# Moving the third weight load behind the last V, one projection layout for all groups, an earlier third K, and an early exponential table: a streamed attention decode step

## The chip, the cores and the metric

One core of one Trainium2 chip. The metric is the device time of the kernel in microseconds (us), as the median of repeated executions. The profile is one execution; its span is some 2 us shorter than the device time (before: span 669.6, time of that execution 671.42). Before: 671.78 us median of 3 runs (671.24 to 672.15).

## The reference, cut to what matters

```python
# B = 4 rows, H = 32 heads, 4096 cached positions, 128 per head, bfloat16
xn = layernorm(x)                                       # (4, 1, 640)
q = (xn @ wq) -> (4, 32, 1, 128)
scores = q . k_cache * 128 ** -0.5                      # k_cache (4, 32, 4096, 128)
o = softmax(scores) . v_cache                           # v_cache the same size
A = o.reshape(4, 1, 4096) @ wo                          # wo (4096, 640)
return x + A + gated_mlp(xn)                            # small weights, done at the start
```

K and V are 134.2 MB each (4 x 32 x 4096 x 128 x 2 bytes). Everything else together is some 14 MB. One core has to read 282 MB, once.

## The kernel before

A **unit** is K or V of 8 heads of one batch row, 8.39 MB. There are 16 units of each; unit u belongs to group u // 4 (8 heads) and batch row u % 4, so group 3, the last, has K12 to K15 and V12 to V15. `wo`, the weights of the output projection, comes in four parts of 1.31 MB, one for each group. One buffer of five slots holds all that is streamed; a unit takes two slots.

```python
seq = [("k", u) for u in range(B)]          # k0 k1 k2 k3, then v0 k4 v1 k5 ... v11 k15 v12 v13 v14 v15
for u in range(NU):
    seq.append(("v", u))
    if u + B < NU:
        seq.append(("k", u + B))
place = {("k", 0): 3, ("k", 1): 0, ("k", 2): 2, ("k", 3): 0}
for u in range(B, NU):
    place[("k", u)] = 1 if u % 2 == 0 else 0
for u in range(NU):
    place[("v", u)] = 3                     # V12 and V14 share slots 3 and 4
place[("v", NU - 3)] = 1                    # V13
place[("v", NU - 1)] = 0                    # V15
first = {2: 1}                              # which half of a K unit is read first
cuts = {("k", 0): (0, T // 2, T), ("k", 1): (0, T // 2, T), ("v", NU - 1): (0, 128, 192, 224, 240, T)}
```

All these loads go out on one queue, in order, from the sync engine. A load into a slot is issued only when the last reader of that slot is done: for a K unit the 8 VectorE transposes, for a V unit the 64 PE matmuls.

```python
# ... the loop that issues everything
for i, item in enumerate(seq):
    if i + 1 < len(seq):
        load_unit(seq[i + 1])
        key, u = seq[i + 1]
        if key == "k" and u >= 2 * B - 1 and u % B == B - 1:
            load_wo(u // B - 1)             # wo of groups 0, 1, 2 behind K7, K11, K15
    else:
        load_wo(NG - 1)                     # wo of group 3 behind V15, in four pieces
    # ... K unit: 8 transposes and their score matmuls; in the last K of a group also
    #     the selection, the transposing and the projection of the group before
    # ... after the last K of a group: softmax(g)
    # ... V unit: emit_V(u); in the last group also emit_selL(b)
emit_proj(state["oL"], last=True)
```

The softmax of a group is a chain over several engines: the maximum, then four times (exponential on ScalarE, 8 transposes of the exponentials `x` on PE), copies `xd` on VectorE, then fills of the matmul weights `Zb` on ScalarE, then the 64 V matmuls of the group's first unit, in two halves. Groups 0 to 2 project through `oh -> om -> oT -> proj`; the last group has a direct, shorter form:

```python
def emit_selL(b):                            # last group: one matmul and one 128x8 multiplication
    oh = misc_ps([P, HG], F32)
    nc.tensor.matmul(oh[:], lhsT=state["R"][:, b, :], rhs=SelH[:], start=True, stop=True)
    nc.vector.tensor_tensor(out=state["oL"][:, :, b], in0=oh[:], in1=state[("rinv", NG - 1)][:, :, b], op=ALU.mult)
```

Of the kernel before, what the change touches and what calls it, by code (L numbers as in the profile page):

```python
# [8 lines left out]
ACT = mybir.ActivationFunctionType  # L9
ALU = mybir.AluOpType  # L10
# [6 lines left out]
def kernel(  # L17
# [19 lines left out]
    nc = tc.nc  # L37
# [90 lines left out]
        place[("v", u)] = 3  # L128
    place[("v", NU - 3)] = 1
    place[("v", NU - 1)] = 0  # L130
    first = {2: 1}
    cuts = {("k", 0): (0, T // 2, T), ("k", 1): (0, T // 2, T), ("v", NU - 1): (0, 128, 192, 224, 240, T)}
    for g in range(NG):
        u = B * g + B - 1
        if u < NU - 1:
            cuts[("k", u)] = (0, T // 2, T)
            first[u] = 0
    for u in range(B, NU):
        if u not in first:
            first[u] = u % 2  # L140

    def unit(item):
# [9 lines left out]
        for t0, t1 in zip(c[:-1], c[1:]):  # L152
            nc.sync.dma_start(out=dst[:, t0 * Dh:t1 * Dh], in_=src[:, t0 * Dh:t1 * Dh])

    wo_v = A_wo.rearrange("(h p) n -> p h n", p=P)

    wo_q = A_wo.rearrange("(g p c) n -> g p c n", p=P, c=HG)
    wo_t = at_slot(2, HG * NOUT).rearrange("p (c n) -> p c n", c=HG)

    def load_wo(g):  # L160
        if g < NG - 1:
            nc.sync.dma_start(out=wo_t, in_=wo_q[g])
        else:
            for h0, h1 in ((0, 4), (4, 6), (6, 7), (7, 8)):
                nc.sync.dma_start(out=wo_t[:, h0:h1, :], in_=wo_v[:, g * HG + h0:g * HG + h1, :])

    load_unit(seq[0])

# [154 lines left out]
    nc.vector.tensor_tensor(out=uT[:, :, 0:B], in0=z1, in1=t1[:], op=ALU.mult)  # L323


    for fc in range(FC):
        n = P if fc < FC - 1 else FL
        nb = B if fc else 32
        for hf in range(NH):
            nc.tensor.matmul(proj[32 * hf:32 * hf + nb, 0:NO2], lhsT=uT[:n, fc, 0:nb],  # L330
                             rhs=w_out[:n, fc, hf * NO2:(hf + 1) * NO2], start=(fc == 0), stop=False)
# [68 lines left out]
    def softmax(g):  # L400
# [22 lines left out]
        z_fill(g, 1)  # L423
        rowsum = small.tile([P, NE], F32, tag="rowsum")
        nc.vector.tensor_reduce(out=rowsum[:], in_=rs[:], axis=AX.X, op=ALU.add)
        if g < NG - 1:
            cs = misc_ps([G, 1], F32)
            for e in range(NE):
                nc.tensor.matmul(cs[:], lhsT=SelPe[:, e].rearrange("p h e b -> p (h e b)"), rhs=rowsum[:, e:e + 1],
                                 start=(e == 0), stop=(e == NE - 1))  # L430
            rinv = small.tile([G, 1], F32, tag="rinv")
            nc.vector.reciprocal(out=rinv[:], in_=cs[:])
        else:
            ds = small.tile([P, HP, NE, B], F32, tag="ds", bufs=1)
            for e in range(NE):
                nc.vector.tensor_scalar(out=ds[:, :, e, :], in0=SelP[:].rearrange("p (h b) -> p h b", b=B),
                                        scalar1=rowsum[:, e:e + 1], scalar2=1.0 / HP, op0=ALU.mult, op1=ALU.mult)
            cs = misc_ps([P, G], F32)
            nc.tensor.matmul(cs[:], lhsT=ones_f[:], rhs=ds[:].rearrange("p h e b -> p (h e b)"), start=True, stop=True)
            rinv = small.tile([P, HG, B], F32, tag="rinvL", bufs=1)  # L440
            nc.vector.reciprocal(out=rinv[:].rearrange("p h b -> p (h b)"), in_=cs[:])
            oL = small.tile([P, HG, B], BF16, tag="oL", bufs=1)
            state["oL"] = oL
        state[("rinv", g)] = rinv

    def emit_V(v):
# [39 lines left out]
        nc.vector.tensor_copy(out=oT[:], in_=oT_ps[:])  # L486
        state[("oT", g)] = oT

    def emit_proj(oT, last=False):
        for c in range(HG):  # L490
            for hf in range(NH):
                nc.tensor.matmul(proj[32 * hf:32 * hf + B, 0:NO2], lhsT=oT[:, c, :],  # L492
                                 rhs=wo_t[:, c, hf * NO2:(hf + 1) * NO2],
                                 start=False, stop=(last and c == HG - 1))

    def emit_selL(b):

        oh = misc_ps([P, HG], F32)
        nc.tensor.matmul(oh[:], lhsT=state["R"][:, b, :], rhs=SelH[:], start=True, stop=True)  # L499
        nc.vector.tensor_tensor(out=state["oL"][:, :, b], in0=oh[:], in1=state[("rinv", NG - 1)][:, :, b], op=ALU.mult)  # L500

    fill_qz(0)
    for i, item in enumerate(seq):
        if i + 1 < len(seq):
            load_unit(seq[i + 1])
            key, u = seq[i + 1]
            if key == "k" and u >= 2 * B - 1 and u % B == B - 1:
                load_wo(u // B - 1)
        else:
            load_wo(NG - 1)  # L510
        key, u = item
        g, b = divmod(u, B)
        if key == "k":
            done = b == B - 1 and g > 0
            for k in range(8):
                emit_K(u, k)
                if done and k == 1:
                    emit_sel(g - 1)
                if done and k == 2:
                    emit_oT(g - 1)  # L520
                if done and k == 5:
                    emit_proj(state.pop(("oT", g - 1)))
            if b == B - 1:
                if g < NG - 1:
                    fill_qz(g + 1)
                softmax(g)
        else:
            emit_V(u)
            if g == NG - 1:
                emit_selL(b)  # L530
    emit_proj(state["oL"], last=True)

    o_bf = const.tile([64, NO2], BF16)
    nc.vector.tensor_copy(out=o_bf[:], in_=proj[:, 0:NO2])
# [31 lines left out]
```

## Time and profile before

| | before |
|---|---|
| time, median (lowest to highest) | 671.78 us (671.24 to 672.15) |
| span of the profiled run | 669.6 us |
| read from HBM | 282.25 MB, 422 GB/s over the span |
| PE / VectorE / ScalarE busy | 46% / 53% / 14% |
| last transpose of K15 ends | 597.27 us |
| V14 issued | 618.13 us, 20.86 after it |
| last V landed | 661.25 us |
| projection ends | 666.68 us |

The lines of the profile behind this stand in the prediction. Idle times of the DMA engines are means over all 16, and times "after K15" count from the end of K15's last transpose. The table is to be read as a line of stations: the stream runs until K15 is in; then the softmax chain of the last group decides when V14 may go into the slots of V12; then the rest of the stream runs; then comes a tail after the last V.

### The profile page before, as it was taken

To read this page: it belongs to the slowest core of one execution; us is meant where nothing else is said; L and a number is where in the kernel's file an instruction comes from. 1 tells how busy PE (TensorE), PEld (TensorE's weight loads), DVE (VectorE), ACT (ScalarE), POOL (GpSimd) and SP (SyncE) were. 2 spreads that over 40 slices of the span, in tenths; PEclk is the share of its full clock that TensorE was granted. 3 is DMA by queue.
4 is the path that set the end of the run, shared out by engine and by line. 5 is a ranking of instruction groups with operands and counts; after the bars stand their busy time and mean duration, and the time that the engine had idled before them with its cause. 6 is when DMAs were issued, how large, how long until landed. Compare 5 with 4: busy or idle time off the path is not lost.

```text
span 669.6 us, 6019 instructions
## 1 busy us (share of the span) xinstructions
PE 304.9 (46%) x2575; PEld 126.4 (19%) x2575; DVE 357.5 (53%) x322; ACT 93.1 (14%) x232; POOL 7.6 (1%) x27
## 2 busy tenths in 40 slices
PE   0656246366054465445436065551706346256244
PEld 0512012132011121221102022230201112013121
DVE  6179499566091658528256286743709165384101
ACT  1100000560200000450200000081020000008300
POOL 1000000000000000000000000000000000000000
PEclk9997878779677587776758596865867758585867
DMA  8999999999999999999999999999999999999995
GB/s 326 430 429 445 413 436 455 388 420 431 412 438 436 438 424 450 435 432 435 428 423 432 438 422 424 459 432 431 431 424 431 439 431 432 438 431 416 400 416 231
DMA packets 8098, 282.64 MB, mean 422 GB/s; under 512 B 916, under 2 KB 2056, under 8 KB 2440
## 3 DMA queue, kind: packets, MB, share of 16 engines
q1 hardware_dynamic: 7976, 282.24, 98.2%
q8 instruction: 20, 0.33, 0.2%
q10 hardware_dynamic: 32, 0.01, 0.0%
q14 instruction: 6, 0.05, 0.0%
q0 software_dynamic: 64, 0.00, 0.0%
HBM read 282.25 MB, written 0.01 MB: 422 GB/s over the span
## 4 chain that ended last, share of the span: by engine, by line
DMA 70%; DVE 14%; issue 12%; ACT 2%; PE 1%; SPq 0%; DVEq 0%; ACTq 0%
DMA kv<-in_A_k_cache_dram 65%; DVE kT L354 12%; DMA kv<-in_A_v_cache_dram 6%; ACT Zb L398 1%; DVE xd L420 1%; ACT p L412 1%; PE O L455 0%; PE proj L492 0%; PE x L416 0%; SPq L115 0%; DVE m L372 0%; PE S L365 0%; DVE R L464 0%; PE misc L377 0%; PE misc L499 0%
## 5 line engine op out<-in xcount | busy, mean ns | idle before, releaser
L354 DVE STREAM_TRANSPOSE kT<-kv 128x2048 f32<-128x2048 f32 x128 | 282.9, 2276 | 143.5 <-DMA kv<-in_A_k_cache_dram 143.5
L365 PE MATMUL S<-kT,QZ 128*32 128x512 bf16 x1024 | 187.9, 500 | 250.0 <-DVE kT L354 250.0
L365 PEld LDWEIGHTS <-QZ 128*32 128x32 bf16 x1024 | 60.5, 111 | 368.9 <-issue 348.8
L455 PE MATMUL O<-kv,Zb 128*32 128x512 bf16 x1024 | 73.3, 440 | 26.2 <-DMA kv<-in_A_v_cache_dram 23.0
L398 ACT ACTIVATE Zb<-xd,MkE 32x256 bf16<-32x256 bf16 (+1 forms) x160 | 65.3, 454 | 95.6 <-PE O L455 87.1
L412 ACT ACTIVATE p<-S,negmax 128x512 bf16<-128x512 f32 x32 | 21.6, 693 | 319.8 <-DVE negmax L386 319.7
L462 DVE TENSOR_SCALAR R<-O,Mk 128x128 f32<-128x128 f32 x16 | 5.6, 351 | 101.6 <-PE O L455 101.6
L455 PEld LDWEIGHTS <-Zb 128*32 128x32 bf16 x1024 | 33.8, 108 | 64.0 <-issue 40.1
L420 DVE COPY xd<-x 32x512 bf16<-32x512 bf16 x32 | 22.0, 687 | 22.5 <-PE x L416 21.7
L416 PE MATMUL x<-IdP,p 128*128 128x128 bf16 x128 | 16.3, 310 | 26.1 <-ACT p L412 16.8
L416 PEld LDWEIGHTS <-p 128*128 128x128 bf16 x128 | 12.4, 141 | 30.4 <-ACT p L412 20.4
L464 DVE SCALAR_TENSOR_TENSOR R<-O,Mk,R 128x128 f32<-128x128 f32 x48 | 16.8, 351 | 1.7
L412 ACT ACT_TABLE_LOAD x1 | 1.3, 1283 | 94.6 <-DVE negmax L386 94.6
L472 PE MATMUL misc<-R,SelR 128*32 128x128 f32 x24 | 4.9, 285 | 19.4 <-DVE R L464 19.4
L341 POOL COPY QZ<-q 32x32 bf16<-32x32 bf16 x16 | 5.1, 320 | 413.5 <-PE S L365 402.3
L265 PE MATMUL misc<-xnT,kv 128*128 128x4 bf16 x160 | 4.4, 166 | 7.4 <-DMA kv<-in_A_wq_dram 7.4
L372 DVE TENSOR_REDUCE m<-S 128x2 f32<-128x1024 f32 x4 | 4.9, 1225 | 4.8 <-PE S L365 4.8
L412 ACT ACTIVATION_READ_ACCUMULATOR p<-S,negmax 128x1 f32 x32 | 6.7, 210 | 0.0
L472 PEld LDWEIGHTS misc<-R,SelR 128*32 128x32 f32 x24 | 1.6, 108 | 25.3 <-DVE R L464 25.3
L377 PE MATMUL misc<-dg,ones_f 128*128 128x256 f32 x8 | 2.7, 416 | 7.5 <-DVE dg L374 7.5
L268 DVE CAST q_bf<-misc 128x128 bf16<-128x128 f32 x1 | 0.3, 291 | 10.9 <-PE misc L265 10.9
L265 PEld LDWEIGHTS <-kv 128*128 128x128 bf16 x160 | 4.3, 104 | 7.5 <-DMA kv<-in_A_wq_dram 7.5
(100 smaller groups left out, 70.5 us busy)
## 6 DMA issues: line engine op xcount, KB each, us to landing
kv<-in_A_k_cache_dram SPq DMA_DIRECT2D x10, 4096.0 KB, 30.2
kv<-in_A_wq_dram SPq DMA_DIRECT2D x1, 5120.0 KB, 17.2
kv<-in_A_v_cache_dram SPq DMA_DIRECT2D x1, 4096.0 KB, 32.8
kv<-in_A_wo_dram SPq DMA_DIRECT2D x3, 1280.0 KB, 28.5
kv<-in_B_w_in_dram SPq DMA_DIRECT2D x1, 2160.0 KB, 21.9
kv<-in_A_v_cache_dram SPq DMA_DIRECT2D x1, 2048.0 KB
kv<-in_A_v_cache_dram SPq DMA_DIRECT2D x1, 1024.0 KB
kv<-in_A_v_cache_dram SPq DMA_DIRECT2D x2, 512.0 KB, 37.3
```

The source lines that it names most:

```text
L265: nc.tensor.matmul(q_ps[:, h, :], lhsT=wq[:, c, h * Dh:(h + 1) * Dh], rhs=xnT[:, c, :], start=(c == 0), stop=(c == DC - 1))
L341: nc.gpsimd.tensor_copy(out=QZ[r0:r0 + 32, :, :, :, 8 + 8 * hp], in_=q3[r0:r0 + 32, :, c0:c0 + NE * B].rearrange("p a (e b) -> p b a e", b=B))
L354: nc.vector.transpose(kT[:].rearrange("p (t r) -> p t r", r=32), kw)
L365: nc.tensor.matmul(S_ps[32 * q:32 * q + 32, e], lhsT=QZ[:, b, 2 * kh + w, e, w0:w0 + 32], rhs=kb[:, i, :, e, :, w], start=(b == 0 and k < ...
L398: nc.scalar.activation(out=dst, in_=src, func=ACT.Copy, scale=MkE[r0:r0 + 32, e:e + 1])
L412: nc.scalar.activation(out=p_q[:, :, :, e, :], in_=S_ps[:, e, 8 * q:8 * q + 8, None, :].to_broadcast((P, 8, HP, M)), func=ACT.Exp, bias=ne ...
L416: nc.tensor.transpose(x[:, 8 * (q % 2) + t, :], p_q[:, t].rearrange("p r e m -> p (r e m)"), IdP[:])
L420: nc.vector.tensor_copy(out=xd[r0:r0 + 32, :, 16 * half:16 * half + 16], in_=x[r0:r0 + 32, :, r0:r0 + 32].rearrange("p t r -> p r t"))
L455: nc.tensor.matmul(O_ps[32 * q:32 * q + 32, :, :], lhsT=Zb[b % 2][:, w].rearrange("p h c -> p (h c)"), rhs=vv[:, w * 4 * Dh:(w + 1) * 4 * ...
L462: nc.vector.tensor_scalar(out=R, in0=O_ps[:, 0, :], scalar1=Mk4[:, 0:1], scalar2=None, op0=ALU.mult)
L464: nc.vector.scalar_tensor_tensor(out=R, in0=O_ps[:, c, :], scalar=Mk4[:, c:c + 1], in1=R, op0=ALU.mult, op1=ALU.add)
L472: nc.tensor.matmul(oh[:], lhsT=SelR[:, b].rearrange("p h b -> p (h b)"), rhs=state["R"][:, b, :], start=(b == 0), stop=(b == B - 1))
```

## The change

The intent: (1) K2 is split, so that half of it lands while VectorE waits for it, and the exponential's table is loaded early; (2) the wo of group 2 no longer stands ahead of V12 in the queue but goes behind the last V, where the tail waits anyway; (3) the last group drops its direct form and projects like the others, whose wo layout moves in longer packets; V15 is cut in three pieces instead of five.

```diff
-    first = {2: 1}
-    cuts = {("k", 0): (0, T // 2, T), ("k", 1): (0, T // 2, T), ("v", NU - 1): (0, 128, 192, 224, 240, T)}
+    first = {}
+    cuts = {("k", u): (0, T // 2, T) for u in range(B - 1)}
+    cuts[("v", NU - 1)] = (0, 128, 224, T)
 ...
-    wo_t = at_slot(2, HG * NOUT).rearrange("p (c n) -> p c n", c=HG)
-    def load_wo(g):
-        if g < NG - 1:
-            nc.sync.dma_start(out=wo_t, in_=wo_q[g])
-        else:
-            for h0, h1 in ((0, 4), (4, 6), (6, 7), (7, 8)):
-                nc.sync.dma_start(out=wo_t[:, h0:h1, :], in_=wo_v[:, g * HG + h0:g * HG + h1, :])
+    wo_t = [at_slot(3 if g == NG - 2 else 2, HG * NOUT).rearrange("p (c n) -> p c n", c=HG) for g in range(NG)]
+    def load_wo(g, c_cuts=(0, HG)):
+        for c0, c1 in zip(c_cuts[:-1], c_cuts[1:]):
+            nc.sync.dma_start(out=wo_t[g][:, c0:c1, :], in_=wo_q[g][:, c0:c1, :])
 ...
+    etab = const.tile([P, 1], F32)
+    nc.scalar.activation(out=etab[:], in_=rs[:, 0:1], func=ACT.Exp)
 ...   # softmax: the row sums of the last group by the same matmuls as the other groups (ds, oL dropped)
 ...   # emit_selL dropped; emit_proj(g, cs) takes the group and a range of heads
-            if key == "k" and u >= 2 * B - 1 and u % B == B - 1:
+            if key == "k" and 2 * B - 1 <= u < NU - 1 and u % B == B - 1:
                 load_wo(u // B - 1)
         else:
-            load_wo(NG - 1)
+            load_wo(NG - 2, (0, 4, 8))
+            load_wo(NG - 1, (0, 4, 6, 7, 8))
 ...
-                if done and k == 5:
-                    emit_proj(state.pop(("oT", g - 1)))
+                if done and k == 5 and g < NG - 1:
+                    emit_proj(g - 1)
 ...
-    emit_proj(state["oL"], last=True)
+    emit_proj(NG - 2, range(0, 4))
+    emit_sel(NG - 1)
+    emit_proj(NG - 2, range(4, HG))
+    emit_oT(NG - 1)
+    emit_proj(NG - 1)
```

More of the change, by code (lines that the diff above doesn't have):

```diff
@@ L136 @@
             cuts[("k", u)] = (0, T // 2, T)
-            first[u] = 0
     for u in range(B, NU):
-        if u not in first:
+        if ("k", u) not in cuts:
             first[u] = u % 2
@@ L153, in load_unit @@
             nc.sync.dma_start(out=dst[:, t0 * Dh:t1 * Dh], in_=src[:, t0 * Dh:t1 * Dh])
-    wo_v = A_wo.rearrange("(h p) n -> p h n", p=P)
     wo_q = A_wo.rearrange("(g p c) n -> g p c n", p=P, c=HG)
-    wo_t = at_slot(2, HG * NOUT).rearrange("p (c n) -> p c n", c=HG)
-    def load_wo(g):
-        if g < NG - 1:
-            nc.sync.dma_start(out=wo_t, in_=wo_q[g])
-        else:
-            for h0, h1 in ((0, 4), (4, 6), (6, 7), (7, 8)):
-                nc.sync.dma_start(out=wo_t[:, h0:h1, :], in_=wo_v[:, g * HG + h0:g * HG + h1, :])
+    wo_t = [at_slot(3 if g == NG - 2 else 2, HG * NOUT).rearrange("p (c n) -> p c n", c=HG) for g in range(NG)]
+    def load_wo(g, c_cuts=(0, HG)):
+        for c0, c1 in zip(c_cuts[:-1], c_cuts[1:]):
+            nc.sync.dma_start(out=wo_t[g][:, c0:c1, :], in_=wo_q[g][:, c0:c1, :])
     load_unit(seq[0])
@@ L425, in softmax @@
         nc.vector.tensor_reduce(out=rowsum[:], in_=rs[:], axis=AX.X, op=ALU.add)
-        if g < NG - 1:
-            cs = misc_ps([G, 1], F32)
-            for e in range(NE):
-                nc.tensor.matmul(cs[:], lhsT=SelPe[:, e].rearrange("p h e b -> p (h e b)"), rhs=rowsum[:, e:e + 1],
-                                 start=(e == 0), stop=(e == NE - 1))
-            rinv = small.tile([G, 1], F32, tag="rinv")
-            nc.vector.reciprocal(out=rinv[:], in_=cs[:])
-        else:
-            ds = small.tile([P, HP, NE, B], F32, tag="ds", bufs=1)
-            for e in range(NE):
-                nc.vector.tensor_scalar(out=ds[:, :, e, :], in0=SelP[:].rearrange("p (h b) -> p h b", b=B),
-                                        scalar1=rowsum[:, e:e + 1], scalar2=1.0 / HP, op0=ALU.mult, op1=ALU.mult)
-            cs = misc_ps([P, G], F32)
-            nc.tensor.matmul(cs[:], lhsT=ones_f[:], rhs=ds[:].rearrange("p h e b -> p (h e b)"), start=True, stop=True)
-            rinv = small.tile([P, HG, B], F32, tag="rinvL", bufs=1)
-            nc.vector.reciprocal(out=rinv[:].rearrange("p h b -> p (h b)"), in_=cs[:])
-            oL = small.tile([P, HG, B], BF16, tag="oL", bufs=1)
-            state["oL"] = oL
+        cs = misc_ps([G, 1], F32)
+        for e in range(NE):
+            nc.tensor.matmul(cs[:], lhsT=SelPe[:, e].rearrange("p h e b -> p (h e b)"), rhs=rowsum[:, e:e + 1],
+                             start=(e == 0), stop=(e == NE - 1))
+        rinv = small.tile([G, 1], F32, tag="rinv")
+        nc.vector.reciprocal(out=rinv[:], in_=cs[:])
         state[("rinv", g)] = rinv
@@ L487, in emit_oT, with emit_proj @@
         state[("oT", g)] = oT
-    def emit_proj(oT, last=False):
-        for c in range(HG):
+    def emit_proj(g, cs=range(HG)):
+        oT = state[("oT", g)]
+        for c in cs:
             for hf in range(NH):
                 nc.tensor.matmul(proj[32 * hf:32 * hf + B, 0:NO2], lhsT=oT[:, c, :],
-                                 rhs=wo_t[:, c, hf * NO2:(hf + 1) * NO2],
-                                 start=False, stop=(last and c == HG - 1))
-    def emit_selL(b):
-        oh = misc_ps([P, HG], F32)
-        nc.tensor.matmul(oh[:], lhsT=state["R"][:, b, :], rhs=SelH[:], start=True, stop=True)
-        nc.vector.tensor_tensor(out=state["oL"][:, :, b], in0=oh[:], in1=state[("rinv", NG - 1)][:, :, b], op=ALU.mult)
+                                 rhs=wo_t[g][:, c, hf * NO2:(hf + 1) * NO2],
+                                 start=False, stop=(g == NG - 1 and c == HG - 1))
     fill_qz(0)
@@ L528 @@
             emit_V(u)
-            if g == NG - 1:
-                emit_selL(b)
-    emit_proj(state["oL"], last=True)
+    emit_proj(NG - 2, range(0, 4))
[3 more added lines that the diff above has]
+    emit_proj(NG - 1)
     o_bf = const.tile([64, NO2], BF16)
```

## The prediction

> **What bounds the kernel now.** I read the page from the top: the slices and the HBM line first, then the chain that ended last, then the timelines of the sync queue and of the last 10 us.
>
> ```profile
> DMA  8999999999999999999999999999999999999995
> GB/s 326 430 429 445 413 436 455 388 420 431 412 438 436 438 424 450 435 432 435 428 423 432 438 422 424 459 432 431 431 424 431 439 431 432 438 431 416 400 416 231
> HBM read 282.25 MB, written 0.01 MB: 422 GB/s over the span
> DMA 70%; DVE 14%; issue 12%; ACT 2%; PE 1%; SPq 0%; DVEq 0%; ACTq 0%
> ```
>
> One slice is 16.7 us. In all but the first and the last the 16 DMA engines are busy over 90%, at about 430 GB/s. 282.25 MB at 430 GB/s are 656 us of the 669.6 us span. So the kernel is a stream, and only what keeps the stream from running (start, gaps, tail) can be won: 13 us, of which the change touches the gaps and the tail. No other engine can bound it: VectorE, the busiest, has 53%.
>
> Gaps. The page's tenths are too coarse for them, so I asked for short stretches around the places where the sync queue waits for the V matmuls. The last two columns are DMA share and GB/s; they count a packet where it starts, and a 64 KB packet lasts 2.4 us, so over a stretch this short only the pattern counts.
>
> ```profile
> core 0: us, PE busy (x) PEld busy (x) DVE busy (x) ACT busy (x) POOL busy (x), PEclk, DMA share, GB/s
> ...
> 616.00:618.00 2.00, 2.00 (x35) 0.66 (x23) 0.00 (x0) 1.95 (x5) 0.00 (x0) 0.86 0.53 229
> 618.00:619.00 1.00, 0.09 (x3) 0.00 (x0) 0.79 (x3) 0.97 (x3) 0.00 (x0) 1.00 0.46 197
> 619.00:620.00 1.00, 0.30 (x2) 0.30 (x2) 0.61 (x2) 0.97 (x3) 0.00 (x0) 1.00 2.38 786
> ```
>
> From 616 to 619 few packets start, then all at once. Packet by packet the trace says: the first engines finish V13 at 616.7 us, the last near 621; V14 is issued at 618.13 and its first packets start at 619.3. Half of the engines idle, 0.83 us on average over 16. A smaller gap of the same kind lies at 141.5 to 142.8 us (V1 waits for V0's matmuls; 0.37 us on average), and some engines run dry at 120 to 124 us, before K4 is issued (about 0.25 us). A gap of 1.5 us at 5.6 us is not touched by the change.
>
> The sync queue around the last group:
>
> ```profile
> 549.84 0.33 SPq L153 DMA_DIRECT2D kv<-in_A_k_cache_dram  x1
> 554.22 0.33 SPq L162 DMA_DIRECT2D kv<-in_A_wo_dram  x1
> 564.81 59.64 SPq L153 DMA_DIRECT2D kv<-in_A_v_cache_dram  x8
> 624.49 32.62 SPq L165 DMA_DIRECT2D kv<-in_A_wo_dram  x4
> ```
>
> The order is K15, wo of group 2, V12, V13, then V14 (618.13), V15 in five pieces, wo of group 3 in four. The tail, from the chain:
>
> ```profile
> 623.97 37.28 DMA kv<-in_A_v_cache_dram
> 661.25 0.04 issue
> 661.29 0.64 PE O L455 x4
> ...
> 663.53 0.61 PE misc L499 x2
> 664.14 0.02 issue
> 664.16 0.19 DVE oL L500
> 664.35 0.04 issue
> 664.39 2.32 PE proj L492 x9
> 666.71 0.02 issue
> 666.73 0.48 DVE o_bf L534
> ```
>
> The last V is in at 661.25 (call it Lv). From there to the end of the projection are 5.46 us, and 2.9 us more to the end of the span (o_bf and the output DMA). wo of group 3 lands behind V at 664.2 and hides under this chain.
>
> **What the Trainium skill says.** "DMA: Bandwidth & Descriptors", section Specifications, gives a fabric ceiling of 435 GB/s; the slices here (mostly 420 to 450; single ones read above the ceiling, the mean of 422 does not) agree that little is left in the stream itself. The same page, Queues, rings and completion order, says each DMA engine consumes descriptors in ring order; that is why wo of group 2, queued between K15 and V12, delays all that follows by its own 1.31 MB. The trace agrees: V13 to V15 come in order behind it. "ScalarE: Activation LUTs", What ACT_TABLE_LOAD costs, has 1283 ns for a load; the trace has 1.28 us, in the softmax of the first group at 125.06 us. "TensorE: Matmul & The Clock Gate", Part 1, says that the PE clock falls back when PE was not busy; here the tail of before ran at a granted 0.50 from 660.9 us on, which sizes my tail below.
>
> **The change, part by part.**
>
> (1) Third K load split, exponential's table early. Before, K2 lands whole at 85.05 us, VectorE having idled 10.9 us for it, and then has 16 transposes in a row to 120.4. The first half of K2 needs only the slot of the first weights, free at about 34 us, so it can land near 75; its four transposes of 2.2 us fill 75 to 84, the next four 85 to 94, and K3 ends with its own second half: landed at 104.46, plus 4 x 2.2 = 113.4. The first softmax starts 7.0 us sooner, and the table load takes 1.28 us off it (the number of table loads stays four). V0's matmuls, which ended at 141.1, end near 133, and K4 can be issued at 113.4 instead of 120.4. Both gaps there close: 0.37 + 0.25 = 0.6 us for everything behind. Not the 8 us: these lie beside the stream.
>
> (2) wo of group 2 moved behind the last V. 1.31 MB at about 415 GB/s are 3.15 us that no longer lie before V12. If the stream had no gap, Lv would come 0.6 + 3.15 = 3.75 us sooner. But V14 goes into the slot of V12, and V12's matmuls wait not for data but for the softmax: 618.13 is 20.85 us after K15's last transpose (597.28), and this distance was 20.1 in groups 1 and 2. K15's landing (579.6) is before wo in the queue, so it moves only by the 0.6 us. V14's first packets then start near 619.3 - 0.6 = 618.7, while V13's bytes run out at 613 to 617.3: all 16 engines idle, about 3.3 us on average instead of 0.83. So the gap takes back 2.5 us of the 3.15. A small return: all engines now start V14 together, where before the last started 1.6 us late. From a clean start, V14 and V15 are 16.78 MB / 430 GB/s = 39.0 us: 618.7 + 39.0 = 657.7, plus 0.5 from last byte to matmul (V15 before: bytes at 660.8, matmul at 661.29), plus 1 for the engines' spread: Lv near 659.5, between 658.9 and 660.3. That is -1.75 us.
>
> (3) The tail. Behind Lv come both wo, 2.62 MB / 0.41 = 6.4 us; the last two matmuls follow 0.5 later: Lv + 6.9. The chain: 8 V matmuls to the first R 0.7, R 1.5 (so Lv + 2.2). PE works in program order: 8 projections of group 2 wait for their half at Lv + 1.6 and take 1.15 (16 took 2.29 at half clock), to Lv + 2.8; the last selection 0.6 (3.4), om 1.27 (4.8), 8 small transposing matmuls and their copy 0.9 (5.8; in group 1 these took 250.68 to 251.56), 16 projections 2.3: Lv + 8.1. At full clock the projections halve (16 in 1.26 at 268.46), the chain gives about 6.8 and the landing decides, Lv + 6.9. Before it was Lv + 5.46. So the tail costs 1.4 to 2.6 us more, 2.0 in the middle. The group now has om (1.27) and oT back that the removed direct form (0.2) did not need; its better packets (rows of 10,240 bytes cut in 2 to 4 pieces instead of 1,280: 388 ns against 8 x 59.8 = 478) win about 0.5 us of landing, in the 6.4 already.
>
> (4) The rowsum matmuls in place of the two scalings, a matmul with ones and a 0.36 us reciprocal: about 0.7 us less on VectorE and PE, but the second half of V12 waits for ScalarE's Zb (615.4, 18.15 us after K15 as in the other groups), so nothing is on the path.
>
> Sum: Lv -1.75, tail +2.0: +0.25 us, with the lower clock +0.85, with the full clock -0.35. V14's issue may come up to 0.7 sooner, since groups 1 and 2 had 20.1 instead of 20.85. Middle: 0. Predicted time 671.8 us.
>
> **Rivals.** (a) The gap does not grow: V13 and its successor keep the queue full and Lv falls the whole 3.75 us; then -3.75 + 2.0 = -1.75, 670.0. For it: groups 1 and 2 have no visible gap. Against it: they have wo in just this place, and the last group has a gap even with it. (b) The tail is worse than its parts: PE at half clock with no overlap of the two halves, or the wo load of group 2 issued late since it waits for V14's matmuls in the same slot. V14's matmuls began at 641.68, 19 us before Lv, so the issue should be in time; if not, +2 to 3, 674. (c) The freed VectorE time of part 1 counts on the path: it would if the first softmax bounded the stream, 7 + 1.28 us, 664. Against it: the DMA share there is above 90% in every slice, so there is no such time to win.
>
> **Range and chances.** The terms of 0.5 to 1.5 us (gap, clock of the tail, spread of engines) add to about 1.3 us either way, and three runs of before span 0.9. 8 in 10: 670.2 to 673.5. 2% is 13.4 us; the whole tail and all gaps together are not that. Faster by over 2%: 0.4%; slower: 0.6%; same: 99%.
>
> **What would show it.** Transposes of K2 starting near 75 us, the first softmax near 113; no gap at 141; V14 issued near 617.5 with a stretch of about 3 us before it in which hardly any packet starts; last V at 659.5; wo landing near 666; projection ending near 667. Wrong: V14 issued before 615, a last V near 657.5, or a projection that ends more than 9 us after the last V.

## The result, and the profile after

The changed kernel takes 672.29 us (671.28 to 674.19, 4 runs); the kernel before, beside it on the same chip, 671.62 us (671.24 to 672.15, 4 runs). The ratio is 1.0013 [0.9989, 1.0036]: the same. A second measurement of the changed kernel on another chip, told below, gave 1.0033 [1.002, 1.0045]: a loss. The profiled spans are 669.6 and 670.7 us.

| station | before | predicted | after |
|---|---|---|---|
| K3 transposed, K4 issued | 120.38 | 113.4 | 113.79 |
| last transpose of K15 ends | 597.27 | 596.7 | 595.38 |
| V14 issued, us after that | 20.86 | at most 20.85 | 22.96 |
| V14 issued | 618.13 | near 617.5 | 618.34 |
| idle of the 16 DMA engines ahead of V14, mean | 0.88 | 3.3 | 5.69 |
| last V landed | 661.25 | 659.5 | 660.99 |
| wo of group 3 landed | 664.66 | near 666 | 667.30 |
| projection ends, us after the last V | 5.43 | 7.5 | 6.73 |
| projection ends | 666.68 | near 667 | 667.72 |

The slices of the page of the changed kernel (DMA share in tenths, and GB/s, 16.8 us each):

```profile
DMA  8999999999999999999999999999999999997996
GB/s 330 422 432 435 426 430 452 434 428 435 434 438 427 426 418 448 434 435 435 430 434 435 430 413 435 444 431 430 427 434 438 431 438 431 434 438 291 419 403 274
```

Two things differ from before. The eighth slice, around 118 to 134 us, is 434 where it was 388: part 1 works. The 37th slice, 604 to 620 us, is 291 where it was 416: a hole. Both, closer. First 116 to 150 us, before and then after; the columns are those of the stretches in the prediction, and the last two are DMA share and GB/s.

```profile
116.00:150.00 34.00, 16.85 (x142) 8.69 (x144) 19.55 (x24) 19.42 (x49) 1.27 (x4) 0.73 0.97 404
```

```profile
116.00:150.00 34.00, 14.16 (x120) 7.34 (x121) 15.16 (x22) 18.13 (x48) 0.44 (x2) 0.61 1.00 432
```

At 34 us, 28 GB/s are 0.95 MB, and at 432 GB/s these are 2.2 us of stream. The station K15 shows 1.9 of them. The prediction had 0.6, the idle time of the engines alone. Packet by packet, the trace of before has 0.72 us of mean idle there; besides, 40 packets of 65,536 bytes (23 in 116 to 130 us, 17 in 140 to 150) took over 2.54 us where the median is 2.42. Their excess over the median, spread over 16 engines, is 1.2 us. The changed kernel has no idle time and no such packet in the same two stretches.

Then the hole, in the changed kernel:

```profile
614.00:616.00 2.00, 1.25 (x12) 0.46 (x16) 0.00 (x0) 1.94 (x5) 0.00 (x0) 0.67 0.00 0
616.00:618.00 2.00, 2.00 (x24) 0.65 (x16) 0.00 (x0) 1.95 (x5) 0.00 (x0) 0.50 0.00 0
618.00:619.00 1.00, 0.29 (x4) 0.00 (x0) 0.62 (x2) 0.60 (x3) 0.00 (x0) 0.95 0.00 0
619.00:620.00 1.00, 0.09 (x1) 0.09 (x2) 0.79 (x3) 0.97 (x3) 0.00 (x0) 1.00 2.72 918
```

No packet starts from 614 to 619 us, then all at once. Meanwhile PE's granted clock is 0.50 (616 to 618 us; 0.86 there before). K15's last transpose and the issue of V14, from the chain and the sync queue (start and time taken), before and then after:

```profile
595.00 2.28 DVE kT L354
618.13 6.32 SPq L153 DMA_DIRECT2D kv<-in_A_v_cache_dram  x6
```

```profile
593.11 2.28 DVE kT L354
618.34 4.14 SPq L153 DMA_DIRECT2D kv<-in_A_v_cache_dram  x4
```

What PE does in between can be read from its timeline (start, busy time, line, operation, count, and in brackets the idle time before and what ended it). Before:

```profile
608.95 1.01 PE L416 MATMUL x<-IdP,p 128*128 128x128 bf16 x8 [3.09 <-DVE xd L420]
610.37 1.03 PE L416 MATMUL x<-IdP,p 128*128 128x128 bf16 x8 [0.41 <-ACT p L412]
611.33 0.61 PE L455 MATMUL O<-kv,Zb 128*32 128x512 bf16 x1
...
612.44 5.65 PE L455 MATMUL O<-kv,Zb 128*32 128x512 bf16 x63
```

After:

```profile
607.35 1.01 PE L416 MATMUL x<-IdP,p 128*128 128x128 bf16 x8 [3.09 <-DVE xd L420]
608.29 1.46 PE L443 MATMUL O<-kv,Zb 128*32 128x512 bf16 x9
609.69 1.03 PE L416 MATMUL x<-IdP,p 128*128 128x128 bf16 x8
...
610.89 1.53 PE L443 MATMUL O<-kv,Zb 128*32 128x512 bf16 x20
614.75 3.54 PE L443 MATMUL O<-kv,Zb 128*32 128x512 bf16 x32 [2.33 <-ACT Zb L398]
```

The order is another one. `x` are the transposes of the exponentials, `O` the matmuls of V12. After, nine matmuls of V12 stand between the third and the fourth set of eight transposes; before, all transposes come first. PE ran its instructions in the order in which the scheduler, the build step that orders each engine's instructions, had put them down, so the last transposes end 15.34 us after K15's last transpose (610.72 less 595.38), where they ended 14.1 after it (611.40 less 597.27). Of these 1.2 us, 0.92 are the nine matmuls: from the third set of transposes to the fourth it is 2.34 us instead of 1.42. The rest arose earlier in the chain: the third set starts 11.97 us after K15 here and 11.68 before, and in other profiles that keep the old order up to 13.14. The copies, the fills and so the second half of V12 start later: 19.37 us after K15's last transpose instead of some 18.2. And that second half, 32 matmuls, took 3.54 us instead of 2.66. Both together make V14's issue 2.1 us later after K15 than before, and eat the 1.9 us that K15 had won. The prediction looked at the order of the tail only; the order of this stretch was to be had before any run.

The tail of the changed kernel, from the timeline of the two engines:

```profile
658.55 3.60 PE L443 MATMUL O<-kv,Zb 128*32 128x512 bf16 x32 [4.45 <-DMA kv<-in_A_v_cache_dram]
662.20 0.35 DVE L450 TENSOR_SCALAR R<-O,Mk 128x128 f32<-128x128 f32 x1 [13.54 <-PE O L443]
...
662.60 0.71 PE L481 MATMUL proj<-kv,oT 128*4 128x320 bf16 x8 [0.45 <-DMA kv<-in_A_wo_dram]
...
664.21 1.27 DVE L463 SCALAR_TENSOR_TENSOR om<-misc,rinv,MkH 32x1024 bf16<-32x1024 f32 x1 [0.50 <-PE misc L460]
...
666.47 1.25 PE L481 MATMUL proj<-kv,oT 128*4 128x320 bf16 x16 [0.28 <-DVE oT L474]
667.77 0.48 DVE L520 CAST o_bf<-proj 64x320 bf16<-64x320 f32 x1 [1.35 <-PE proj L481]
```

The last V piece lands at 660.99, while PE still works at half clock through the 24 matmuls of the piece before it; the 8 last ones follow without a pause. `om` and `oT` (1.27 us, and 0.65 and 0.19 behind it) are the detour of the common layout. The 16 projections took 1.25 us, at full clock. Wo had landed at 667.30, and the last two of them started at 667.42 at the pace of those before, so it was the chain through `om` and `oT` that decided the end, with 0.1 us to spare on the stream.

So far: from before to after the last V comes 0.26 us sooner and the tail is 1.30 us longer, together +1.04, which is the difference of the projection ends and, to a hundredth, of the spans.

### The profile page after: what moved, and what is told of

Same layout as the page of the kernel before. It is cut to its first block, busy times and chain, and to the rows that moved or that the text cites. A ratio compares the mean times of both kernels' runs of the same rounds, so it can differ in the third digit from the quotient of the medians.

```text
span 670.7 us, 6034 instructions
## 1 busy us (share of the span) xinstructions
PE 305.4 (46%) x2585; PEld 126.8 (19%) x2585; DVE 357.8 (53%) x318; ACT 93.3 (14%) x233; POOL 8.0 (1%) x27
## 4 chain that ended last, share of the span: by engine, by line
DMA 73%; DVE 11%; issue 11%; PE 3%; ACT 1%; DVEq 0%; SPq 0%; ACTq 0%
DMA kv<-in_A_k_cache_dram 65%; DVE kT L354 9%; DMA kv<-in_A_v_cache_dram 5%; DMA kv<-in_A_wq_dram 3%; PE O L443 1%; PE misc L261 1%; DVE xd L420 1%; ACT Zb L398 0%; PE x L416 0%; ACT p L412 0%; DVE R L452 0%; DVE om L463 0%; PE proj L481 0%; DVE m L372 0%; PE S L365 0%
## 5 line engine op out<-in xcount | busy, mean ns | idle before, releaser
L365 PE MATMUL S<-kT,QZ 128*32 128x512 bf16 x1024 | 190.1, 505 | 245.8 <-DVE kT L354 245.8
L443 PE MATMUL O<-kv,Zb 128*32 128x512 bf16 x1024 | 70.4, 428 | 32.1 <-DMA kv<-in_A_v_cache_dram 26.8
L452 DVE SCALAR_TENSOR_TENSOR R<-O,Mk,R 128x128 f32<-128x128 f32 x48 | 16.8, 351 | 1.7
L460 PE MATMUL misc<-R,SelR 128*32 128x128 f32 x32 | 6.5, 285 | 24.7 <-DVE R L452 24.7
L481 PE MATMUL proj<-kv,oT 128*4 128x320 bf16 x64 | 7.0, 370 | 0.8 <-DMA kv<-in_A_wo_dram 0.5
L463 DVE SCALAR_TENSOR_TENSOR om<-misc,rinv,MkH 32x1024 bf16<-32x1024 f32 x4 | 5.1, 1272 | 2.0 <-PE misc L460 2.0
```

Of the source, the lines that this page charges most:

```text
L365: nc.tensor.matmul(S_ps[32 * q:32 * q + 32, e], lhsT=QZ[:, b, 2 * kh + w, e, w0:w0 + 32], rhs=kb[:, i, :, e, :, w], start=(b == 0 and k < ...
L443: nc.tensor.matmul(O_ps[32 * q:32 * q + 32, :, :], lhsT=Zb[b % 2][:, w].rearrange("p h c -> p (h c)"), rhs=vv[:, w * 4 * Dh:(w + 1) * 4 * ...
L452: nc.vector.scalar_tensor_tensor(out=R, in0=O_ps[:, c, :], scalar=Mk4[:, c:c + 1], in1=R, op0=ALU.mult, op1=ALU.add)
L460: nc.tensor.matmul(oh[:], lhsT=SelR[:, b].rearrange("p h b -> p (h b)"), rhs=state["R"][:, b, :], start=(b == 0), stop=(b == B - 1))
L481: nc.tensor.matmul(proj[32 * hf:32 * hf + B, 0:NO2], lhsT=oT[:, c, :], rhs=wo_t[g][:, c, hf * NO2:(hf + 1) * NO2], start=False, stop=(g == ...
```

## The experiments

The theory after reading the traces: **(T)** part 1 wins some 1.9 us of stream; the moved wo wins nothing, because V14 waits for the softmax chain and not for bytes; the changed order on PE makes this wait longer; the long layout costs in the tail. The rivals: **(R1)** the wo move is a gain and only the layout spoils it; **(R2)** the order of the instructions does not matter, the hole is just the 1.31 MB that are missing ahead of V14; **(R3)** the moved wo gains nothing even without the hole, since its bytes lie before the end wherever they stand. The kernel before was timed beside each batch: 672.14, 672.19 and 671.24 us.

**Part 1 alone.**

```diff
-    first = {2: 1}
+    first = {}
-    cuts = {("k", 0): (0, T // 2, T), ("k", 1): (0, T // 2, T), ...
+    cuts = {("k", 0): (0, T // 2, T), ("k", 1): (0, T // 2, T), ("k", 2): (0, T // 2, T), ...
+    nc.scalar.activation(out=etab[:], in_=rs[:, 0:1], func=ACT.Exp)
```

> The kernel before with the third K load split and the exponential's table loaded early, nothing else. Theory (the stream only loses its own gaps there): the first softmax starts 7 us sooner, the gap at 141 us is gone, K15's last transpose ends 0.6 us (predicted) to 1.9 us (as in the changed kernel, 595.39 against 597.28) sooner, V14 is issued about 20.1 to 20.9 us after it with a gap as before; time -0.6 to -1.9 us, 669.7 to 671. Rival (the first softmax bounds the stream): -7 to -8 us, 664. Rival (the 1.9 us are chance of one profile): K15's end within 0.5 us of before, time unchanged.

Measured: 670.27 us, 0.9972 [0.9959, 0.9985]. V14 is issued at 616.71, 20.84 us after K15's last transpose, the distance of before. Part 1 is a gain of 1.9 us by the time (1.0 to 2.8 by the interval), and it reaches the end. In this profile K15 was 1.41 us sooner than before (595.86). One profile gives such a station to a microsecond only: the three without part 1 have it at 596.99 to 597.38, eight of the nine with part 1 at 594.99 to 595.95, and the ninth, of a run told below, at 597.35, already 1.1 us behind the change when K3 was transposed.

**The change with wo of group 2 back in its old place** (so part 1 and the common layout).

```diff
-    wo_t = [at_slot(3 if g == NG - 2 else 2, ...
+    wo_t = [at_slot(2, ...
-            if key == "k" and 2 * B - 1 <= u < NU - 1 and u % B == B - 1:
+            if key == "k" and 2 * B - 1 <= u and u % B == B - 1:
-            load_wo(NG - 2, (0, 4, 8))
-                if done and k == 5 and g < NG - 1:
+                if done and k == 5:
-    emit_proj(NG - 2, range(0, 4))
-    emit_proj(NG - 2, range(4, HG))
```

> The changed kernel with wo of group 2 loaded between K15 and V12 again and projected during K15, as before; split K load, early table and the common layout stay. Theory (the moved wo was the filler of the gap, and its move also let the scheduler put nine V12 matmuls ahead of the last score transposes): the gap before V14 falls from 5.5 us to under 1.5 us, V14 is issued 20.1 to 20.9 us after K15's last transpose (22.95 in the changed kernel), last V near 659.5, tail after it about 1 us longer than before for om and oT, time 670.5 to 671.5, about 1 us under the changed kernel. Rival (the move is neutral): time as the changed kernel, 672.3, or 1 us more.

Measured: 672.34 us, 1.0000 [0.9988, 1.0013]. The expectation missed by a microsecond, and the time is the one that the rival named (672.3): the layout costs more than I gave it. That the move is not neutral all the same is seen in the trace. The distance to V14 is 20.81 us and the idle time ahead of it 1.16 us, so the hole and the new order do come with the moved wo. The price of the layout shows in the tail. This kernel, then part 1 alone, from the timelines:

```profile
662.78 0.35 DVE L450 TENSOR_SCALAR R<-O,Mk 128x128 f32<-128x128 f32 x1 [12.71 <-PE O L443]
...
667.28 2.30 PE L481 MATMUL proj<-kv,oT 128*4 128x320 bf16 x16 [0.28 <-DVE oT L474]
```

```profile
660.56 0.35 DVE L465 TENSOR_SCALAR R<-O,Mk 128x128 f32<-128x128 f32 x1 [12.23 <-PE O L458]
...
662.99 2.30 PE L495 MATMUL proj<-kv,oL 128*4 128x320 bf16 x16 [0.27 <-DVE oL L503]
```

From the first R to the first projection it is 4.50 us through `om` and `oT`, 2.43 directly; the projections take the same 2.30. That is 2.07 us more in the traces; the ratios differ by 0.28% of 672, or 1.9 us. The two profiles differ by more than that, 4.30 us at the end of the projection: this one is the slowest of its six runs (674.38, median 672.34), its last V landed 1.71 us later (661.56 against 659.85), and from there to the first R it took 1.22 us instead of 0.71, with V15 in larger pieces. So the detour fits the price by size; no run has it alone. Wo itself landed at 664.70 here, long before the last projections began, so the chain decides the end and the layout has to be paid.

**The moved wo alone** (the direct form of the last group kept).

```diff
+    wo_ts = [at_slot(3 if g == NG - 2 else 2, ...) for g in range(NG)]
-            if key == "k" and u >= 2 * B - 1 and u % B == B - 1:
+            if key == "k" and 2 * B - 1 <= u < NU - 1 and u % B == B - 1:
+            load_wo(NG - 2)            # two pieces, behind the last V
+    emit_proj(state.pop(("oT", NG - 2)), NG - 2)
```

> The kernel before with only the wo of group 2 moved behind the last V; no split K, no early table, the direct form for the last group. Theory: the static order has the nine V12 matmuls early here too; V14 is issued 22 to 23 us after K15's last transpose (597.3), so near 620, with a gap of 5 to 6 us on average; the last V lands 1 to 2 us later than before, 662 to 663; both wo land 6.4 us behind it; time 673.5 to 675. Rival (the move alone gains what it takes out of the stream, 3.15 us, less 1.4 of tail): 670. Rival (neutral): 671.6.

Measured: 673.96 us, 1.0029 [1.0013, 1.0044]. So the move by itself, as it is scheduled, is a loss, and R1 falls. The order on PE is the new one here too, without any of the other parts: it is the moved load with its projection that changes it. The engines idle 3.77 us on average ahead of V14, wo lands at 668.03, and the projection ends at 668.61. The time was as expected; the trace was milder than that, 21.56 us to V14 instead of 22 to 23 and 3.77 of idle time instead of 5 to 6, and the last V landed at 661.44, only 0.2 later than before.

**The change with V12's matmuls put behind the last transposes.** Only the order in which PE is given its instructions differs; data and waits are the same. The edit holds for the first V of every group, not only V12; K15 came no sooner by it (595.86).

```diff
-                    nc.tensor.transpose(x[:, ...], ...)
+                    state["xlast"] = nc.tensor.transpose(x[:, ...], ...)
-            emit_V(u)
+            if b == 0:
+                with tc.issue_after(state["xlast"]):
+                    emit_V(u)
+            else:
+                emit_V(u)
```

> The changed kernel with one thing forced: the matmuls of a group's first V are queued behind all score transposes (issue order alone; no wait added). Theory: V14 is issued 20.1 to 20.9 us after K15's last transpose instead of 22.95, the gap shrinks from 5.5 us to about 3.3 us (the prediction's figure), last V about 2 us sooner, time 670 to 671. Rival (the distance of 22.95 is the half clock alone, not the order): still 22 or more, time 672.

Measured: 670.75 us, 0.9976 [0.9963, 0.9989], where the change itself was 1.0013 and 1.0033 (each against the kernel before on its own chip). R2 falls: the order alone is worth between 0.37 and 0.57% (2.5 to 3.8 us). From PE's timeline of this kernel:

```profile
610.97 2.52 PE L443 MATMUL O<-kv,Zb 128*32 128x512 bf16 x29
614.83 1.91 PE L443 MATMUL O<-kv,Zb 128*32 128x512 bf16 x32 [1.34 <-ACT Zb L398]
```

The second half of V12 takes 1.91 us, and V14 is issued 20.92 us after K15's last transpose, as before. The 2.04 us against the change (22.96) are 0.93 of the nine matmuls and 1.63 of the faster second half, less 0.52 by which this chain was behind at the third set of transposes. The idle time ahead of V14 is still 4.13 us: the order was an accident on top of the hole, not the hole. Against wo in its old place (1.0000) the move now gains 0.24%, or 1.6 us. Where this comes from is not shown: `om` and `oT` stand on the chain that ended last here as well, and of the two profiles the one of wo in its old place was the slow one told of above. Part 1 alone had 0.9972 without move or layout.

**The change with the first half of V15 loaded ahead of V14.** The slot of that half is free as soon as K15 is transposed, so it can fill the hole.

```diff
+            if seq[i + 1] == ("v", NU - 2):
+                load_unit(("v", NU - 1), slice(0, 1))
-            load_unit(seq[i + 1])
+            load_unit(seq[i + 1], slice(1, None) if seq[i + 1] == ("v", NU - 1) else None)
```

> The changed kernel with one thing moved: the first half of V15, whose slot is free as soon as K15 is transposed (595.4), is queued ahead of V14, so 4.19 MB (9.75 us) fill the gap while V14 waits for V12's matmuls. Theory (the gap of 5.5 us is where the moved wo's gain went): no gap at 612 to 620, stream about 5 us earlier behind it, last wo landing near 662, projection ending near 662.5 to 663.5 (667.74 in the changed kernel), time 667.5 to 669. Rival (the gap does not count, the end is set by VectorE and PE of the last group): V14's matmuls still end last, time within 1 us of the changed kernel's 672.3.

Measured: 667.37 us, 0.9927 [0.9914, 0.994], a little better than expected (667.5 to 669). Its ratio is the best, though three kernels below are not told apart from it, and it beats the kernel before and the change. Its stretches where the change had its hole:

```profile
614.00:616.00 2.00, 0.69 (x8) 0.30 (x12) 0.32 (x2) 1.92 (x6) 0.00 (x0) 0.73 0.95 410
616.00:618.00 2.00, 2.00 (x24) 0.81 (x20) 0.00 (x0) 1.95 (x5) 0.00 (x0) 0.50 0.99 426
```

V14 is issued no sooner than in the change (618.74), but the engines work on V15 meanwhile. The tail of this kernel:

```profile
660.97 1.64 PE L481 MATMUL proj<-kv,oT 128*4 128x320 bf16 x16 [0.28 <-DVE oT L474]
662.65 0.48 DVE L522 CAST o_bf<-proj 64x320 bf16<-64x320 f32 x1 [1.73 <-PE proj L481]
```

Wo lands at 662.26 and the projection ends 0.35 us later: its last two matmuls waited for that landing, so now the stream alone decides.

**The same filling of the hole in the kernel before.**

> The kernel before with the first half of V15 queued ahead of V14, nothing else. Theory: only the small gap at 617 to 619 (0.83 us on average) is there to be closed; time -0.8 to -1.3 us against before, so much less than the same edit gives the changed kernel (-4). Rival (loading V15 early has a worth of its own, in the tail): -3 or more here too.

Measured: 669.93 us, 0.9967 [0.9951, 0.9983]: 2.2 us, more than the 0.8 to 1.3 expected. The profiled run was the slowest of the six (671.25), with 0.6 us more idle time around 140 us than before had, so the traces can be compared only locally: across the hole, the stream of the filled kernel gains 1.43 us on that of before. As at 120 us, that is more than the idle time that was filled (0.88 us); the 65,536-byte packets around it that ran long made up 0.6 more. But this gain does not reach the end of the stream in the profile: wo landed at 664.91, against 664.66 before, and the 16 engines finish less together: from 650 us to the last packet of wo they idle 2.1 us on average, before 1.0. So the 2.2 us are shown by the time alone (interval 1.1 to 3.3), and no trace accounts for them in full.

**The same filling with part 1 alone.**

> The kernel before with the split K load, the early table and V15's first half ahead of V14; wo of group 2 stays ahead of V12, direct form for the last group. Theory: the two gains add, -1.9 and -1, time 668.7 to 669.5, no gap left after the start.

Measured: 667.81 us, 0.9935 [0.992, 0.995], 0.9 us better than the expectation's best: the two gains (1.9 and 2.2 by the times) add. With the hole filled, the moved wo and the common layout together take the ratio from 0.9935 to 0.9927, which the intervals do not separate. The six runs of this kernel lie within 0.9 us, those of the change with the hole filled within 0.3; those of the kernel before on the same chip within 3.1.

The end of this kernel is, narrowly, no longer the stream's: wo had landed at 662.66, and the last two matmuls started at 662.76 at the pace of those before. From its timeline:

```profile
649.04 7.72 PE L458 MATMUL O<-kv,Zb 128*32 128x512 bf16 x89 [22.13 <-DMA kv<-in_A_v_cache_dram]
...
657.20 2.34 PE L458 MATMUL O<-kv,Zb 128*32 128x512 bf16 x39
...
659.58 0.35 DVE L465 TENSOR_SCALAR R<-O,Mk 128x128 f32<-128x128 f32 x1 [2.10 <-PE O L458]
```

V14 now lands behind half of V15, so PE sits idle for 22 us until it is there and then does it and V15 in one go, to 659.5. The engines are also further apart: the first of the 16 finished its part of V14 at 643.93, the last at 648.90, 5.0 us later; in the kernel before these were 2.0 us apart (639.54, 641.55). A load has landed only when the last engine is done.

**Part 1, the moved wo, the direct form, the order mended and the hole filled.** What R3 is about: the best that the move could give.

> The kernel before with the split K load, the early table, wo of group 2 behind the last V, V15's first half ahead of V14, score transposes ahead of V12's matmuls, and the direct form and the five-piece cut of the last group kept. Theory: with the gap closed the moved wo is worth what the plan wanted: last V near 655.5, the projection then ends with the landing of the last wo piece near 662, time about 667, 1.5 to 2 us under part1_v15first. Rival (the moved wo gains nothing even without the gap, since the stream ends at the same time and the tail after it is as long): the same as part1_v15first within 0.7 us.

Measured: 668.10 us, 0.9938 [0.9925, 0.9952]. Wo lands at 662.34, against 662.26 in the change with the hole filled and 662.66 with part 1 alone and the hole filled, where the wo of group 2 is still in its old place. The three landings lie within 0.4 us of each other, and the projections end 0.69, 0.35 and 0.40 us behind them. Only in the second did the last matmuls wait for wo; here the 16 projections started late, on an earlier piece of wo, and took 2.29 us at half clock. The rival named in the expectation (within 0.7 us of part 1 alone with the hole filled) came true, so R3 is right by time and by landing: with the queue full, moving 1.31 MB from the middle to the end of it moves nothing. The part of T that says this is only because of the hole has to be widened.

**The change once more, beside the next three.**

> The changed kernel itself, for a direct comparison in the rounds of this call: time within 1 us of before (ratio 1.000 to 1.003), gap before V14 of 4.5 to 6 us. Rival: a difference over 2 us either way would mean that the earlier single comparison was chance.

Measured: 673.46 us, 1.0033 [1.002, 1.0045]. Both figures lie just outside the expectation (1.000 to 1.003, and 4.5 to 6 us for the hole): the change is a loss of 2.2 us beside these runs of the kernel before. That is over the 2 us at which the rival would call the first comparison (0.9 us) chance; the two intervals overlap, so both can hold. The hole is 6.75 us, V14 comes 23.45 us after K15, and this time the tail meets the half clock:

```profile
667.32 2.30 PE L481 MATMUL proj<-kv,oT 128*4 128x320 bf16 x16 [0.28 <-DVE oT L474]
```

The last V landed at 661.85, the projection ended at 669.61: 7.76 us, a tail that is 2.3 longer than before's. With 1.25 us for the same 16 projections in the first profile, this is the run-to-run spread of the changed kernel.

**Only K2 split; only the early table.**

```diff
+ first = {}, cuts with ("k", 2): (0, T // 2, T)        # one kernel
+ nc.scalar.activation(out=etab[:], in_=rs[:, 0:1], func=ACT.Exp)   # the other kernel
```

> The kernel before with only the third K load split (no early table). Theory: V0's matmuls end 7 us sooner, no gap at 120 to 145; the whole gain of part 1, -1.5 to -1.9 us. Rival (both halves of part 1 needed): the gap at 141 us stays in part, gain under 1 us.

> The kernel before with only the exponential's table loaded early. Theory: the first softmax loses 1.28 us, V1 is issued at 139.8 instead of 141.1, so the gap at 141.5 shrinks or closes, the dry engines at 120 to 124 stay: gain 0.3 to 1.2 us. Rival (hidden): no gain, since K4's late issue at 120.4 is what costs.

Measured: 670.24 us, 0.9992 [0.998, 1.0005], and 671.5 us, 0.9997 [0.9984, 1.001]. Both expectations missed (1.5 to 1.9 and 0.3 to 1.2 us of gain): neither is told from before by its time, so the time does not share out part 1's gain. In the traces K15's last transpose comes 1.06 and 1.15 us sooner, and then V14 comes late (21.53 and 22.31 us after it), with 1.84 and 1.90 us of idle time ahead of it, so the gain is given back. The longer distance with the old order is again PE's pace: the second half of V12 took 2.80 and 2.64 us, in part 1 alone 1.91, and with the table alone the chain was 0.7 us behind already at its last transposes (15.59 us after K15 against 14.86). What slowed PE there stays open. The table alone also brought the idle time of 116 to 150 us down to some 0.1 us, though K4 was still issued at 120; yet 23 of the long packets remained, so these do not need a dry spell.

**The change with the hole filled and the order mended.**

> The changed kernel with V15's first half ahead of V14 and the score transposes ahead of V12's matmuls. Theory (once the gap is closed V14 has 10 us of slack, so the order of V12's matmuls no longer counts): 667.4, the same as without the forced order within 0.4 us. Rival (the order is worth its 1.6 us on top): 665.8.

Measured: 667.24 us, 0.9944 [0.9932, 0.9956], as expected. This is another chip, on which the kernel before was faster (671.24), so by the ratio it is 0.9944 against 0.9927, with intervals that overlap. With the hole filled, no gain from the order of PE is seen: the DMA engines have no idle time ahead of V14, which was issued at 618.27.

## Why the prediction was right or wrong

The range held: 672.29 us against 671.8, in 670.2 to 673.5. The reason it gave, that the moved wo turns into a longer gap ahead of V14 and a longer tail, is what the runs show. But the middle came out right because errors of opposite sign cancelled.

1. **The sum.** Lv, the landing of the last V, −1.75 and the tail +2.0 were predicted; −0.26 and +1.30 were measured. The miss of 1.5 us in the first term is partly covered by 0.7 in the second.
2. **Part 1** ("Both gaps there close: 0.37 + 0.25 = 0.6 us for everything behind") was mis-sized: 1.9 us at K15. The times of K2 (transposes from 75.79), K4 (issued at 113.79) and the first softmax (its first maximum 6.6 us sooner) came as predicted. What failed was to take a gap for the idle time of the engines: packets beside it ran long and cost 1.2 us more. Part 1 alone agrees in the time (1.9, interval 1.0 to 2.8).
3. **The gap ahead of V14** failed in its first step, "618.13 is 20.85 us after K15's last transpose (597.28), and this distance was 20.1 in groups 1 and 2", which was carried over. The distance became 22.96, because the scheduler put nine matmuls of V12 ahead of the last transposes (0.9 us) and because the second half of V12 ran slower (3.54 us instead of 2.66); the run with the order mended has 20.92. Hence V14 at 618.34: 1.3 us sooner by part 1 than predicted, 2.1 later by the distance. The gap of 5.69 us is the predicted 3.3, plus the 1.3 by which the bytes ran out sooner, plus the 0.84 by which V14 came later, to 0.25 us. The refill behind it took 42.65 us to Lv where 42.0 were predicted.
4. **The tail** was +2.0 in the middle, between +1.4 at full clock and +2.6 at half. The two profiles have +1.30 at full clock and +2.3 at half: the size held, the middle was a guess between two states. One step did not: at full clock the landing was to decide, and it was the chain that did (6.73 us behind the last V, wo 6.31). Its terms: both wo landed 6.31 us after the last V, predicted 6.4; the first R started 1.21 us after it instead of 0.7, since V15's larger pieces left PE with 32 matmuls in a row at half clock.
5. **Rival (c)**, that part 1's time on VectorE counts in full (664), was rightly thrown out. Rival (a), that the gap does not grow (670.0), was also wrong as it was put; filling the hole gives even less time (667.37), but not for the reason of that rival: without the move it is 667.81. Of rival (b), the half clock came in one of the two profiles; its late issue did not (both wo were issued from 642.65 to 651.21, ahead of the last V).
6. **Small slips in its sums**, none of which changes the result: 104.46 and four transposes of 2.2 are 113.3, not 113.4; 657.7 + 0.5 + 1 is 659.2, not 659.5; and the terms of the half-clock chain add to Lv + 7.9, not 8.1 (measured 7.76).

Accounting by kernels, each against before: part 1 −1.9 us; the common layout on top +1.9 (with the old wo place); the moved wo on top of these +0.9 to +2.2, which is −1.6 from the move with the order mended (cause not shown) and +2.5 to +3.8 from the order on PE. With the hole filled, the last two together are worth −0.4 us, not separated from zero.

Open: why the second half of V12 takes 3.38 to 3.54 us in three of four profiles with the changed order looked at (1.91 in the fourth, the moved wo alone), and 1.91 to 2.80 otherwise. A longer pause of PE before it, 2.33 us against 1.34 in the two timelines above, would fit, but five profiles with hardly any pause (0.03 us) had 2.56 to 2.80, and no run isolates it. Open too is why packets run long there, and why the engines are further apart when the hole is filled.

## What to carry to other kernels

Where one in-order queue bounds a kernel and is full, moving bytes within it moved nothing here; look for the places where the queue waits for a buffer, and put a load there whose buffer is already free (here half a V unit, −0.7%). A load that stands ahead of such a wait may be what hides it, so ask what the wait will cost before taking the load away. After any change compare the static order of every engine over the whole program, not just where the diff is: moving one load with its projection put nine matmuls into the middle of a chain that the queue waits for.

## What the Trainium skill lacked or had wrong

- "DMA: Bandwidth & Descriptors", section Measured, has rates for transfers by size, but nothing on a queue that runs dry for a moment. Here a dry spell of 0.72 us (mean over the engines) came with 40 packets over 2.54 us instead of 2.42, together 1.9 us of stream; one of 0.88 us ahead of V14 cost 1.4 across the hole. Nor has the page a figure for how far apart the 16 engines finish one load: 2.0 us at V14 before, 5.0 with part 1 and the hole filled. Its section Specifications agrees: 435 GB/s as the ceiling, 432 measured over 116 to 150 us with no dry spell.
- "ScalarE: Activation LUTs", What ACT_TABLE_LOAD costs, adds some 1380 ns of drain to a load of 1283 ns, 2.66 us in all. In the trace of before the maximum ended at 124.98, the load ran from 125.06 to 126.34 and the first exponential started at 126.36: the load of 1.28 us is there, a drain of that size is not. ScalarE had been idle for 94.6 us there; but in the changed kernel too, where a load ran from 30.29 to 31.57 right behind an activation that ended at 30.27, the next one started at 31.58. Taking the load off the path alone gave no gain that the time can show (0.9997).
- "TensorE: Matmul & The Clock Gate", Part 1, says that the state of the clock varies from run to run, but not how to size a tail of short bursts: the same 16 projections of the same kernel took 1.25 us in one profile and 2.30 in another, a spread of 1 us at the end of the path.
- No page says that moving a load or a projection can change the order that the scheduler gives to another part of the program: here worth 0.37 to 0.57%, by the change with and without the order mended.
